# First weight pair turned between the first attention steps, and the second MLP's first product in front of the first MLP's last units

## The chip, the cores and the metric

One core of a Trainium2 chip. The metric is device time of one execution in microseconds (us); the table below has the median of 3 runs. Engines are named as the profile names them: PE is TensorE (PEld its weight loads), DVE is VectorE, ACT is ScalarE, POOL is GpSimd, SP is SyncE, which issues all transfers here.

## The reference

Three stages follow each other: a block-wise linear attention with decay (2 batches, 8 heads, 768 positions, 12 blocks of 64), an MLP (512 to 2048 to 512, leaky ReLU), and a second MLP (512 to 1024 to 512) with a SoLU and a layer norm in the middle. There are 1536 tokens.

```python
# attention, for each block b of 64 positions
intra = np.einsum('bhic,bhjc->bhij', qb, kb) * Dmask[None]
intra = np.einsum('bhij,bhjd->bhid', intra, vb)
inter = np.einsum('bhid,bhde->bhie', qb * lam_pow[None], kv_state)
out[:, :, sl] = intra + inter
kv_state = lam_block[None, :, None, None] * kv_state + np.einsum('bhsd,bhse->bhde', kb * rev_pow[None], vb)
...
# first MLP
h = x @ w_in
x = np.maximum(0.01 * h, h) @ w_out
...
# second MLP
h = x @ w_in
e = np.exp(h - h_max)
solu = h * e / (np.sum(e, axis=-1, keepdims=True) + 1e-09)
ln = (solu - mu) / np.sqrt(var + 1e-06) * g_ln
return ln @ w_out
```

The weights are of a wider type than float32 in memory; the host only regroups their bytes.

## The kernel before

**Numbers in two parts.** Every product of the MLPs is made of three: high part by high part, high by low, low by high. The activations lie in SBUF as `xhi`, `xlo` for each of three blocks of 512 tokens, the weights as tiles `wio` (first MLP), `wa`, `wb` (second MLP) with a high and a low half.

**Weights.** They arrive as raw 64-bit words (`raww`), in pairs: pair n holds column group n of `w_in` (IN) and row group n of `w_out` (OUT) of the first MLP, 512 KB each. Turning a pair into float32 parts takes four helpers: `words(n)` (two ACT operations), `convert(n)` (three DVE operations), `high(n)` (one ACT operation that rounds to the high part) and `low(n)` (one DVE subtraction). Each may be called for one half, IN or OUT.

**Attention.** There are 12 steps of one block of 64 positions for both batches. Step s has its loads (`load_step`, five transfers, 1 MB), products of scores (`scores_mm`), their mask (`scores_ev`, DVE), the new state (`scale_k`, `state_mm`, `state_ev`, with `decay_state` on POOL), the scaled queries (`scale_q`, POOL, one buffer `qs`), and the output product (`x_mm`), whose result goes to `xhi` (`x_hi`, ACT) and `xlo` (`x_lo`, DVE). Steps 0 to 3 come first and fill block 0 of the tokens; steps 4 to 11 are spread over the first MLP.

**First MLP.** A loop over 48 items: 3 blocks of tokens by 16 column groups. Item i has its first product `l1_mm` (12 matmuls into `hps`), `l1_split` (ACT: leaky ReLU in place, rounding to `ghi`; DVE: `glo`) and its second product `l2_mm` (12 matmuls into the four `acc` banks). The second product of item i - 1 stands behind the first product of item i. During items 1 to 15 the weight pairs are turned too, up to three pairs ahead. After the last item of a block, `l2_split` moves `acc` to `xhi`, `xlo`.

**Second MLP.** A loop over 12 tiles of 128 tokens: `h2_mm` (24 matmuls into two banks), `h2_norm` (maximum, ACT's exponential, DVE's products and statistics, POOL's power, DVE's last scaling: tile `e`), `ln_transpose` (8 transposes into `acc` 0 and 1), `ln_split` (ACT `lnhi`, DVE `lnlo`), and `out_mm` (24 matmuls, into `acc` 2 or 3, then a copy and a store).

**What sets the order.** Each engine runs its instructions in the order in which the code is written: at the end of the function every instruction is tied to the one before it on its engine. So all that stands ahead of a waiting instruction on its engine's list delays it. Every transfer is issued by SP, in order. PSUM has eight banks: four `acc`, two `hps`, and two that belong to attention (`aps`) and, when attention is over, to the second MLP (`bps`).

Of the kernel before, what the change touches and what calls it, by code (L numbers as in the profile page):

```python
# [16 lines left out]
P = 128  # L17
# [24 lines left out]
def fused_kernel(ctx: ExitStack, tc: tile.TileContext, att, vt, tab, cst, w_in, w_out, w_in2, w_out2, out):  # L42
# [184 lines left out]
    def load_weights(n):  # L227
        if n >= len(order):
            return
        kind, f = key = order[n]  # L230
        t = wp.tile([P, 2, 512, 2], U32, tag="w", name="raww")
        if kind == "a":
            sync.dma_start(out=t.rearrange("p h a b -> p (h a b)"), in_=w_in2[f].bitcast(U32))
        else:
            for i, src in enumerate((w_in[f], w_out[f]) if kind == "io" else (w_out2[f], w_out2[f + 1])):
                sync.dma_start(out=t[:, i].rearrange("p a b -> p (a b)"), in_=src.bitcast(U32))
                if n == 0 and i == 0:
                    load_step(NPRE - 1)
# [95 lines left out]

    et, lnt = {}, {}

    def h2_banks(t):
        return hps if t % 2 == 0 else bps

    def h2_mm(t):  # L340
        b, o = divmod(t * P, NBLK)
# [5 lines left out]
                        bank, x[b][:, k, o : o + P], w[:, s], start=(k == 0 and i == 0), stop=(k == KD - 1 and i == 2)  # L347
                    )

    def h2_norm(t, between):  # L350

        banks = h2_banks(t)
        small = sp.tile([P, 24], F32, tag="small", name="small")
# [65 lines left out]
    zero = cp.tile([P, CH], F32, name="zero")  # L419
    pool.memset(zero, 0.0)  # L420
    sync.dma_start(out=tabs, in_=tab)
    for s in range(NPRE - 1):
        load_step(s)
    for n in range(NLEAD):
        load_weights(n)
    load_step(NPRE)
    sync.dma_start(out=fix, in_=cst)
# [14 lines left out]
    scores_mm(0)  # L442
    scores_ev(0)
    state_mm(0, hps)
    state_ev(0, hps)
    x_mm(0, xb[0])
    x_hi(0, xb[0])
    x_lo(0, xb[0])

    scale_q(1, pool)  # L450
    decay_state(1, pool)
    scale_k(1, pool)
    scores_mm(1)
    scores_ev(1)
    x_mm(1, xb[1])
    state_mm(1, hps)
    x_hi(1, xb[1])
    x_lo(1, xb[1])
    state_ev(1, hps)

    decay_state(2, pool)
    scale_q(2, pool)
    scale_k(2, pool)
    scores_mm(2)
    scores_ev(2)
    x_mm(2, xb[0])
    state_mm(2, hps)
    x_hi(2, xb[0])
    words(0, IN)
    x_lo(2, xb[0])  # L470
    state_ev(2, hps)
    convert(0, IN)
    decay_state(3, pool)

    scale_q(3, pool)
    scores_mm(3)
    high(0, IN)
    low(0, IN)
    scores_ev(3)
    l1_mm((0, 0), hps[0], 0, 256)  # L480
    words(0, OUT)
    convert(0, OUT)
    x_mm(3, xb[1])
    x_hi(3, xb[1])
    x_lo(3, xb[1])
    high(0, OUT)
    low(0, OUT)
    l1_mm((0, 0), hps[0], 256, 512)
    scale_k(3, pool)
    state_mm(3, aps)  # L490
    words(1, IN)
    convert(1, IN)
    l1_split((0, 0), hps[0])
    state_ev(3, aps)
    decay_state(4, pool)
    l2_mm((0, 0))
    words(1, OUT)
    high(1, IN)
    low(1, IN)
    convert(1, OUT)  # L500
    words(2)
    high(1, OUT)
    low(1, OUT)
# [16 lines left out]
    for i, u in enumerate(items[1:], 1):  # L520
        bank = hps[i % 2]
        l1_mm(u, bank)
        s = step_at.get(i)
        before = step_at.get(i - 1)
        if s is not None:
            scale_k(s, pool)
            scale_q(s, pool)
            scores_mm(s)
        if before is not None:
            state_ev(before, aps)  # L530
            decay_state(before + 1, pool)
            x_mm(before, aps)
        l1_split(u, bank)
        high(pair_at(i, 1))
        low(pair_at(i, 1))
        if s is not None:
            scores_ev(s)
        if before is not None:
            x_hi(before, aps)
            x_lo(before, aps)  # L540
            load_step(before + 1)
        if i == 1:
            words(3)
# [94 lines left out]
```

## Time and profile before

| | us |
|---|---|
| Time, median of 3 runs | 493.92 (493.74 to 494.28) |
| Profiled execution, its own time | 494.47 |
| Its span in the trace | 492.7 |
| TensorE busy | 463.0 (94%) |
| VectorE busy | 259.5 (53%) |
| ScalarE busy | 182.4 (37%) |
| GpSimd busy | 51.1 (10%) |

The span is from the first to the last instruction; 1.8 us lie around it. Busy shares are means over all stages: the first 50 us hold four attention steps and the turning of the first weights, where several engines take turns; the rest is nearly all matmuls. A row of a list in time order gives the start, the length, engine, line, operation, output and inputs; in brackets is the idle time of the engine before it and what ended it.

### The profile page before, as it was taken

The numbers are of one execution on the slowest core, as the hardware profiler recorded it, in microseconds if no ns is written. First come the engines' busy times: TensorE is split into PE (matmuls) and PEld (weight loads), VectorE is DVE, ScalarE is ACT, GpSimd is POOL, SyncE is SP. The second block draws the span as 40 slices with busy tenths as digits, with TensorE's granted clock in tenths as the row PEclk, the third lists the DMA queues.
The fourth block names the chain that finished last, engine by engine and source line by source line (L and its number), as shares of the span: only waits on it lengthen the run. The fifth ranks groups of instructions, "written<-read, shape, count | busy, mean of one in ns | idle before, by whom it ended". The sixth has DMA issues, their size and how long they took to land.

```text
span 492.7 us, 7879 instructions
## 1 busy us (share of the span) xinstructions
PE 463.0 (94%) x3344; PEld 373.2 (76%) x3344; DVE 259.5 (53%) x412; ACT 182.4 (37%) x295; POOL 51.1 (10%) x61
## 2 busy tenths in 40 slices
PE   7474999999999999999999999999879999999997
PEld 4463777777787777777888888888658888888886
DVE  3568788788834121121131598913675666555661
ACT  2155846656423212121233677612312222222221
POOL 2603021302210202010000000000000000000000
PEclk9978899999999999999999999999989999999999
DMA  7995045634200202020005552000000000000001
GB/s 238 370 381 226 1 119 225 216 130 169 76 13 1 86 1 86 1 86 1 1 1 173 211 209 91 0 0 1 1 1 21 21 23 21 33 33 23 21 23 43
DMA packets 20243, 41.61 MB, mean 84 GB/s; under 512 B 1904, under 2 KB 11632, under 8 KB 19696
## 3 DMA queue, kind: packets, MB, share of 16 engines
q1 hardware_dynamic: 20208, 41.11, 23.8%
q8 instruction: 26, 0.43, 0.4%
q14 instruction: 9, 0.07, 0.0%
HBM read 37.95 MB, written 3.15 MB: 83 GB/s over the span
## 4 chain that ended last, share of the span: by engine, by line
PE 85%; DMA 7%; DVE 4%; issue 1%; ACT 1%; SPq 1%; POOL 0%; ACTq 0%
PE hps L311 27%; PE acc L327 27%; PE acc L404 14%; PE hps L346 6%; PE bps L346 6%; DMA raww<-in_w_out_dram 2%; DMA ld<-in_att_dram 2%; PE acc L382 2%; PE aps L187 2%; DMA raww<-in_w_in_dram 1%; PE aps L201 1%; DMA ldw<-in_att_dram 1%; PE aps L150 1%; PE aps L166 1%; DVE x L263 1%
## 5 line engine op out<-in xcount | busy, mean ns | idle before, releaser
L311 PE MATMUL hps<-xhi,wio 128*128 128x512 f32 (+1 forms) x392 | 132.8, 400 | 11.6 <-ACT wio L283 10.8
L318 DVE TENSOR_TENSOR glo<-hps,ghi 128x512 fp32r<-128x512 f32 x48 | 33.2, 691 | 126.7 <-ACT ghi L317 126.7
L327 PE MATMUL acc<-ghi,wio 128*128 128x512 f32 x384 | 97.4, 396 | 0.7 <-ACT ghi L317 0.7
L311 PEld LDWEIGHTS hps<-xhi,wio 128*128 128x128 f32 x392 | 75.0, 193 | 29.8 <-ACT wio L283 11.4
L314 ACT ACTIVATE hps<-hps 128x512 f32<-128x512 f32 x48 | 27.9, 582 | 150.1 <-PE hps L311 150.1
L327 PEld LDWEIGHTS acc<-ghi,wio 128*128 128x128 f32 x384 | 70.8, 188 | 16.7 <-ACT ghi L317 0.8
L311 PE MATMUL hps<-xlo,wio 128*128 128x512 f32 (+1 forms) x196 | 77.3, 395 | 0.1
L327 PE MATMUL acc<-glo,wio 128*128 128x512 f32 x192 | 51.4, 389 | 0.0
L404 PE MATMUL acc<-wb,lnhi 128*128 128x512 f32 (+1 forms) x208 | 48.7, 388 | 0.3 <-ACT lnhi L390 0.3
L311 PEld LDWEIGHTS hps<-xlo,wio 128*128 128x128 f32 x196 | 38.0, 194 | 7.8 <-DVE xlo L219 0.3
L404 PEld LDWEIGHTS acc<-wb,lnhi 128*128 128x128 f32 x208 | 37.4, 194 | 7.4 <-ACT lnhi L390 0.6
L327 PEld LDWEIGHTS acc<-glo,wio 128*128 128x128 f32 x192 | 36.0, 188 | 7.6
L263 DVE SCALAR_TENSOR_TENSOR x<-x,raww 128x1024 uint32<-128x1024 uint32 (+1 forms) x26 | 32.3, 1241 | 0.9
L374 POOL TENSOR_TENSOR small<-small,nhalf 128x1 f32<-128x1 f32 x12 | 6.6, 550 | 251.8 <-DVE small L373 251.8
L262 DVE SCALAR_TENSOR_TENSOR raww<-x,raww 128x1024 uint32<-128x1024 uint32 (+1 forms) x26 | 30.7, 1182 | 1.4 <-ACT raww L253 0.3
L346 PE MATMUL hps<-wa,xhi 128*128 128x512 f32 x96 | 30.2, 396 | 0.0
L346 PE MATMUL bps<-wa,xhi 128*128 128x512 f32 x96 | 30.1, 395 | 0.0
L391 DVE TENSOR_TENSOR lnlo<-acc,lnhi 128x512 fp32r<-128x512 f32 x24 | 15.5, 686 | 26.8 <-ACT lnhi L390 26.8
L317 ACT CAST ghi<-hps 128x512 fp32r<-128x512 f32 x48 | 28.2, 588 | 1.5
L253 ACT ACTIVATE raww<-raww 128x1024 uint32<-128x1024 uint16 (+1 forms) x26 | 28.0, 1077 | 0.0
L252 ACT ACTIVATE x<-raww 128x1024 f32<-128x1024 f32 (+1 forms) x26 | 27.9, 1074 | 0.0
L404 PE MATMUL acc<-wb,lnlo 128*128 128x512 f32 (+1 forms) x104 | 24.0, 373 | 0.0
(80 smaller groups left out, 500.5 us busy)
## 6 DMA issues: line engine op xcount, KB each, us to landing
raww<-in_w_out_dram SPq DMA_DIRECT2D x24, 512.0 KB, 6.5
raww<-in_w_in_dram SPq DMA_DIRECT2D x16, 512.0 KB, 7.0
raww<-in_w_in_dram SPq DMA_DIRECT2D x4, 1024.0 KB, 4.8
ld<-in_att_dram SPq DMA_DIRECT2D x8, 384.0 KB, 4.2
ld<-in_att_dram SPq DMA_DIRECT2D x24, 128.0 KB, 4.0
out_dram<-osb SPq DMA_DIRECT2D x11, 256.0 KB, 2.0
ld<-in_vt_dram SPq DMA_DIRECT2D x8, 256.0 KB, 3.7
ldw<-in_att_dram SPq DMA_DIRECT2D x4, 384.0 KB, 5.2
```

Of the source, the lines that this page charges most:

```text
L252: act.activation(x, raw[:, :, 1].bitcast(F32), AF.Copy, scale=HI_SCALE)
L253: act.activation(raw[:, :, 0], raw.bitcast(U16)[:, :, 1], AF.Copy, scale=LO_SCALE)
L262: dve.scalar_tensor_tensor(raw[:, :, 0], xu, 3, raw[:, :, 0], op0=ALU.logical_shift_left, op1=ALU.bitwise_or)
L263: dve.scalar_tensor_tensor(xu, xu, 0x80000000, raw[:, :, 0], op0=ALU.bitwise_and, op1=ALU.bitwise_or)
L311: pe.matmul(bank[:, c0:c1], w[:, s, k], x[b][:, k, c0:c1], start=(i == 0), stop=(i == len(terms) - 1))
L314: act.activation(bank, bank, AF.Prelu, alpha=0.01)
L317: act.copy(ghi, bank)
L318: dve.tensor_tensor(glo, bank, ghi.bitcast(F32), op=ALU.subtract)
L327: pe.matmul(acc[m], w[:, s, m], g, start=(f == 0 and first), stop=(f == NF - 1 and last))
L346: pe.matmul(bank, x[b][:, k, o : o + P], w[:, s], start=(k == 0 and i == 0), stop=(k == KD - 1 and i == 2))
L391: dve.tensor_tensor(lo[:, part], src, hi[:, part].bitcast(F32), op=ALU.subtract)
L404: pe.matmul(po[:, 0:n], x[:, k], w2_t["b", k][:, s, cols], start=(i == 0), stop=(i == len(terms) - 1))
```

## The change

Three things are moved; apart from the first product of item 0, which was in two parts of 256 tokens and is now in one of 512, and from `scale_k(1)`, which goes from POOL (two operations) to ACT (eight), no operation is added or removed.

1. Weight pair 0 is loaded behind step 0, ahead of steps 1 to 3 (before: its first half behind step 2, its second behind step 3).
2. The front is written in another order. Pair 0 is turned between steps 0 and 2, and pair 1 between steps 2 and 3 and behind them. `x_mm(2)` stands behind `scores_mm(3)`. Item 0's second product goes behind item 1's first.
3. The second MLP's first product of token tile 0 stands behind the second product of item 45, and its `h2_norm` behind the split of item 47. The bank pairs `hps` and `bps` change places (tile 0 uses `bps`). In the loop over tiles the output product stands ahead of the transposes, and the norm ahead of `ln_split` of the tile before; the last tile keeps the old order.

```diff
@@ load_weights
-                if n == 0 and i == 0:
-                    load_step(NPRE - 1)
@@ h2_banks
-        return hps if t % 2 == 0 else bps
+        return bps if t % 2 == 0 else hps
@@ loads
-    for s in range(NPRE - 1):
+    load_step(0)
+    load_weights(0)
+    for s in range(1, NPRE):
         load_step(s)
-    for n in range(NLEAD):
+    for n in range(1, NLEAD):
         load_weights(n)
@@ the front
     state_mm(0, hps)
+    x_mm(0, xb[0])
     state_ev(0, hps)
-    x_mm(0, xb[0])
+    words(0, IN)
     x_hi(0, xb[0])
+    words(0, OUT)
+    convert(0, IN)
     x_lo(0, xb[0])
+    decay_state(1, pool)
+    high(0, IN)
 
     scale_q(1, pool)
-    decay_state(1, pool)
-    scale_k(1, pool)
+    scale_k(1, act)
     scores_mm(1)
     scores_ev(1)
     x_mm(1, xb[1])
     state_mm(1, hps)
+    low(0, IN)
+    convert(0, OUT)
     x_hi(1, xb[1])
+    high(0, OUT)
     x_lo(1, xb[1])
     state_ev(1, hps)
...
     scores_ev(2)
-    x_mm(2, xb[0])
+    low(0, OUT)
     state_mm(2, hps)
...
+    words(1, IN)
 
     scale_q(3, pool)
     scores_mm(3)
...
+    x_mm(2, xb[0])
     scores_ev(3)
...
+    state_ev(2, hps)
+    decay_state(3, pool)
+    x_hi(2, xb[0])
+    words(1, OUT)
+    convert(1, IN)
+    x_lo(2, xb[0])
     x_mm(3, xb[1])
     x_hi(3, xb[1])
     x_lo(3, xb[1])
...
+    high(1, IN)
+    low(1, IN)
     scale_k(3, pool)
+
+    l1_mm((0, 0), hps[0])
     state_mm(3, aps)
...
+    convert(1, OUT)
+    words(2)
     l1_split((0, 0), hps[0])
+    high(1, OUT)
+    low(1, OUT)
     state_ev(3, aps)
     decay_state(4, pool)
-    l2_mm((0, 0))
...
     convert(2)
@@ the loop over items
-        if i > 1:
-            l2_mm(items[i - 1])
-            if items[i - 1][1] == NF - 1:
-                l2_split(items[i - 1][0])
+        if i == len(items) - 1:
+            h2_norm(0)
+        l2_mm(items[i - 1])
+        if items[i - 1][1] == NF - 1:
+            l2_split(items[i - 1][0])
         if s is not None:
             state_mm(s, aps)
+        if i == last:
+            att_psum.close()
+            pb = ctx.enter_context(tc.tile_pool(name="pb", bufs=1, space=bass.MemoryType.PSUM))
+            bps.extend(pb.tile([P, 512], F32, name=f"bps{j}") for j in range(2))
+        if i == len(items) - 2:
+            h2_mm(0)
@@ the loop over tiles
-    for t in range(NT):
+    for t in range(1, NT):
         h2_mm(t)
-        if t >= 1:
+        if t < NT - 1:
+            h2_norm(t)
+            if t >= 2:
+                out_mm(t - 2)
             ln_transpose(t - 1)
-        h2_norm(t, (lambda: ln_split(t - 1)) if t >= 1 else (lambda: None))
-        if t >= 2:
+            ln_split(t - 1)
+        else:
+            ln_transpose(t - 1)
+            h2_norm(t, lambda: ln_split(t - 1))
             out_mm(t - 2)
```

ScalarE's list at steps 0 and 1 (`state` and `xhi` belong to attention, `x`, `raww` and `wio` to weight pair 0, `ldw` to step 1's keys), as a piece of the difference:

```order
 L174 COPY state<-hps_87 128x256
+L250 ACTIVATE x<-raww 128x512
+L251 ACTIVATE raww<-raww 128x512
 L215 CAST xhi_92<-acc_82 128x4x64
 L215 CAST xhi_92<-acc_83 128x4x64
+L250 ACTIVATE x<-raww 128x512
+L251 ACTIVATE raww<-raww 128x512
+L281 CAST wio<-x 128x512
+L130 ACTIVATE ldw<-ldw,dmask 128x64 x8
 L215 CAST xhi_92<-acc_84 128x4x64
 L215 CAST xhi_92<-acc_85 128x4x64
```

The words of pair 0, its first rounding and the scaled keys stand now around the outputs of steps 0 and 1.

VectorE's list from step 2's state (`state`, its last part) to the rest of pair 1, after the change:

```order
L177 TENSOR_TENSOR state<-hps_87,sd 128x256
L259 TENSOR_SCALAR x<-x 128x512
L260 SCALAR_TENSOR_TENSOR raww<-x,raww 128x512
L261 SCALAR_TENSOR_TENSOR x<-x,raww 128x512
L219 TENSOR_TENSOR xlo_95<-acc_82,xhi_92 128x4x64
L219 TENSOR_TENSOR xlo_95<-acc_83,xhi_92 128x4x64
L219 TENSOR_TENSOR xlo_95<-acc_84,xhi_92 128x4x64
L219 TENSOR_TENSOR xlo_95<-acc_85,xhi_92 128x4x64
L299 TENSOR_TENSOR wio<-x,wio 128x512
```

`convert(1, IN)` stands ahead of the low parts of steps 2 and 3; before, the first half of pair 0 stood in this place, and between the two steps.

VectorE's list at the end of the first MLP, before (`glo` of item 47, then `l2_split` of block 2, then the norm of tile 0):

```order
L318 TENSOR_TENSOR glo<-hps_87,ghi 128x512
L332 TENSOR_TENSOR xlo_97<-acc_82,xhi_94 128x512
L332 TENSOR_TENSOR xlo_97<-acc_83,xhi_94 128x512
L332 TENSOR_TENSOR xlo_97<-acc_84,xhi_94 128x512
L332 TENSOR_TENSOR xlo_97<-acc_85,xhi_94 128x512
L359 TENSOR_REDUCE small<-hps_86 128x1
```

and after:

```order
L375 TENSOR_SCALAR small<-small 128x1
L376 TENSOR_SCALAR e<-e,small 128x1024
L330 TENSOR_TENSOR xlo_97<-acc_82,xhi_94 128x512
L330 TENSOR_TENSOR xlo_97<-acc_83,xhi_94 128x512
L330 TENSOR_TENSOR xlo_97<-acc_84,xhi_94 128x512
L330 TENSOR_TENSOR xlo_97<-acc_85,xhi_94 128x512
L359 TENSOR_REDUCE small<-hps_86 128x1
```

The whole norm of tile 0, up to `e`, has moved ahead of the four `xlo` pieces; behind them the norm of tile 1 begins, which now uses `hps`.

## Rows read from the trace of the kernel before

**Rows 1.** The page, busy time of each engine over the span.
```profile
PE 463.0 (94%) x3344; PEld 373.2 (76%) x3344; DVE 259.5 (53%) x412; ACT 182.4 (37%) x295; POOL 51.1 (10%) x61
```

**Rows 2.** TensorE in time order: start, length, what; gap before it and releaser.
```profile
25.49 0.58 PE L311 MATMUL hps<-xhi,wio 128*128 128x256 f32 x1 [4.55 <-ACT wio L283]
...
47.72 0.79 PE L311 MATMUL hps<-xhi,wio 128*128 128x512 f32 x1 [6.27 <-ACT wio L283]
...
55.22 0.40 PE L311 MATMUL hps<-xhi,wio 128*128 128x512 f32 x1
```

**Rows 3.** Stretches: length, busy time by engine (instructions), granted clock, DMA share, GB/s.
```profile
21.00:24.50 3.50, 0.00 (x0) 0.00 (x0) 3.38 (x4) 0.00 (x0) 3.03 (x3) 1.00 1.02 413
...
45.00:51.50 6.50, 3.78 (x9) 3.01 (x10) 5.62 (x7) 4.88 (x5) 0.00 (x0) 0.50 0.00 0
...
362.50:365.80 3.30, 3.30 (x10) 2.52 (x9) 1.19 (x4) 2.41 (x6) 0.00 (x0) 0.50 0.00 0
```

**Rows 4.** An issue of SP, its us to landing (last), the next transfer's landing.
```profile
15.42 0.43 SPq L236 DMA_DIRECT2D raww<-in_w_in_dram  x1
...
raww<-in_w_in_dram SPq DMA_DIRECT2D x1, 512.0 KB, 7.3
...
17.08 6.90 DMA raww<-in_w_out_dram
```

**Rows 5.** ScalarE (ACT) in time order, the first 55 us.
```profile
20.10 0.68 ACT L253 ACTIVATE raww<-raww 128x512 uint32<-128x512 uint16 x1
...
34.38 0.58 ACT L314 ACTIVATE hps<-hps 128x512 f32<-128x512 f32 x1 [0.53 <-PE hps L311]
...
46.62 1.04 ACT L283 CAST wio<-x 128x1024 fp32r<-128x1024 f32 x1 [2.78 <-DVE x L263]
```

**Rows 6.** VectorE (DVE) in time order, the first 55 us.
```profile
21.24 0.42 DVE L261 TENSOR_SCALAR x<-x 128x512 f32<-128x512 f32 x1
...
23.15 1.63 DVE L263 SCALAR_TENSOR_TENSOR x<-x,raww 128x512 uint32<-128x512 uint32 x1
...
26.92 0.41 DVE L261 TENSOR_SCALAR x<-x 128x512 f32<-128x512 f32 x1
...
28.15 0.69 DVE L263 SCALAR_TENSOR_TENSOR x<-x,raww 128x512 uint32<-128x512 uint32 x1
...
36.22 0.68 DVE L177 TENSOR_TENSOR state<-aps,sd 128x512 f32<-128x512 f32 x1
...
43.38 0.69 DVE L261 TENSOR_SCALAR x<-x 128x1024 f32<-128x1024 f32 x1
...
45.36 1.23 DVE L263 SCALAR_TENSOR_TENSOR x<-x,raww 128x1024 uint32<-128x1024 uint32 x1
```

**Rows 7.** GpSimd (POOL) in time order, 36 to 42 us.
```profile
36.98 1.06 POOL L142 TENSOR_TENSOR sd<-state,qpow 128x512 f32<-128x512 f32 x1 [11.13 <-DVE state L177]
38.00 1.83 POOL L132 TENSOR_TENSOR ld<-ld,dmask 128x256 f32<-128x256 f32 x2
39.80 1.74 POOL L120 TENSOR_TENSOR qs<-ld,qpow 128x512 f32<-128x512 f32 x1
```

**Rows 8.** Second MLP's start: a stretch, TensorE's, VectorE's lists, the chain of waits.
```profile
338.66:369.48 30.82, 26.01 (x114) 20.71 (x113) 21.31 (x47) 7.84 (x20) 1.11 (x2) 0.94 0.00 1
...
361.47 1.09 PE L382 MATMUL acc<-fix,e 128*128 128x128 f32 x8 [3.23 <-DVE e L376]
...
338.80 2.48 DVE L332 TENSOR_TENSOR xlo<-acc,xhi 128x512 fp32r<-128x512 f32 x4 [3.47 <-ACT xhi L331]
...
350.69 0.81 DVE L376 TENSOR_SCALAR e<-e,small 128x1024 f32<-128x1024 f32 x1
...
375.22 0.87 PE acc L382 x8
376.10 5.48 PE acc L404 x24
381.57 5.58 PE hps L346 x24
```

More of the change, by code (lines that the diff above doesn't have):

```diff
@@ L335, in fused_kernel @@
     et, lnt = {}, {}
+    bps = []
     def h2_banks(t):
-        return hps if t % 2 == 0 else bps
+        return bps if t % 2 == 0 else hps
     def h2_mm(t):
@@ L348, in h2_mm, with h2_norm @@
                     )
-    def h2_norm(t, between):
+    def h2_norm(t, between=lambda: None):
         banks = h2_banks(t)
@@ L456, in fused_kernel @@
     state_mm(1, hps)
+    low(0, IN)
+    convert(0, OUT)
     x_hi(1, xb[1])
+    high(0, OUT)
     x_lo(1, xb[1])
     state_ev(1, hps)
-    decay_state(2, pool)
     scale_q(2, pool)
     scale_k(2, pool)
+    decay_state(2, pool)
     scores_mm(2)
     scores_ev(2)
-    x_mm(2, xb[0])
+    low(0, OUT)
     state_mm(2, hps)
[L468 to L473, printed above, removed]
+    words(1, IN)
     scale_q(3, pool)
     scores_mm(3)
-    high(0, IN)
-    low(0, IN)
+    x_mm(2, xb[0])
     scores_ev(3)
-    l1_mm((0, 0), hps[0], 0, 256)
-    words(0, OUT)
-    convert(0, OUT)
+    state_ev(2, hps)
[4 more added lines that the diff above has]
+    x_lo(2, xb[0])
     x_mm(3, xb[1])
@@ L485, in fused_kernel @@
     x_lo(3, xb[1])
-    high(0, OUT)
-    low(0, OUT)
-    l1_mm((0, 0), hps[0], 256, 512)
+    high(1, IN)
+    low(1, IN)
     scale_k(3, pool)
+    l1_mm((0, 0), hps[0])
     state_mm(3, aps)
-    words(1, IN)
-    convert(1, IN)
+    convert(1, OUT)
+    words(2)
     l1_split((0, 0), hps[0])
+    high(1, OUT)
+    low(1, OUT)
     state_ev(3, aps)
     decay_state(4, pool)
-    l2_mm((0, 0))
[L497 to L503, printed above, removed]
     convert(2)
@@ L549, in fused_kernel @@
         load_weights(pair_at(i, 5))
-        if i > 1:
-            l2_mm(items[i - 1])
-            if items[i - 1][1] == NF - 1:
-                l2_split(items[i - 1][0])
+        if i == len(items) - 1:
[3 more added lines that the diff above has]
+            l2_split(items[i - 1][0])
         if s is not None:
             state_mm(s, aps)
+        if i == last:
[4 more added lines that the diff above has]
+            h2_mm(0)
     l2_mm(items[-1])
     l2_split(items[-1][0])
-    att_psum.close()
-    pb = ctx.enter_context(tc.tile_pool(name="pb", bufs=1, space=bass.MemoryType.PSUM))
-    bps = [pb.tile([P, 512], F32, name=f"bps{i}") for i in range(2)]
     NT = NTOK // P
-    for t in range(NT):
+    for t in range(1, NT):
         h2_mm(t)
-        if t >= 1:
+        if t < NT - 1:
+            h2_norm(t)
+            if t >= 2:
+                out_mm(t - 2)
             ln_transpose(t - 1)
-        h2_norm(t, (lambda: ln_split(t - 1)) if t >= 1 else (lambda: None))
-        if t >= 2:
+            ln_split(t - 1)
+        else:
+            ln_transpose(t - 1)
+            h2_norm(t, lambda: ln_split(t - 1))
             out_mm(t - 2)
```

## The prediction

> **What bounds the kernel now.** The page's first lines come first: the matrix engine is busy 463.0 of 492.7 us [rows 1], so a change of order can give back at most what lies in its gaps and in the time it works at half clock. Next the list of the matrix engine in time order, for the gaps. Two stand at the front: 4.55 us before the first product of block 0 (25.49) and 6.27 us before item 2 (47.72), both released by ScalarE rounding a turned weight to `wio` (line 283) [rows 2]. The granted clock of the stretch at 45.0 to 51.5 is 0.50, the lower of its two levels (1.2 of 2.4 GHz), and at 362.5 to 365.8 too [rows 3]: in both places a gap of some us went ahead. From 55.22 on, where item 3 starts, the front is over; I use that start as the mark of the front. The second place is the start of the second MLP: from the first product's start at 338.66 to the fourth's at 369.48 it takes 30.82 us, with the matrix engine busy 26.01 and a gap of 3.23 us that waits for VectorE's normalised `e` [rows 8]. Between these two places and behind them nothing waits long, and the change touches it only by a swap of order.
>
> **The end: second MLP's first product early.** Three first products (5.58 each), two transposes (0.87 each) and one output product (5.48) [rows 8] are 16.74 + 1.74 + 5.48 = 23.96 us of work at full clock. The stretch takes 30.82, so 6.86 are lost there. Now token tile 0's product stands two units earlier, and its normalisation runs beside the last units. Counted from its start at 0, with 0.2325 us a matmul (5.58 / 24): product to 5.6, item 47's first product (12 matmuls, 2.8) to 8.4, its `glo` 1.9 later at 10.3 (34.38 to 36.22 is this distance for item 0 [rows 5, 6]). Behind that VectorE normalises tile 0. Before, from the product's end (338.66 + 5.58 = 344.24) to the end of the last step (350.69 + 0.81 = 351.50) that took 7.26 us [rows 8], so `e` stands at 17.5; the four `xlo` pieces of `l2_split` behind it take 2.48, and the two that the transposes' banks wait for are done at 18.8. The matrix engine needs them after two second products (2.8 each) and tile 1's first product (5.58): 8.4 + 5.6 + 5.6 = 19.6. Cover left: 0.8 us. Next, VectorE starts tile 1's norm at 20.0 and ends it at 27.3, then `ln_split(0)` (two of about 0.65) at 28.6. The output product of tile 0 now starts at 19.6 + 0.9 + 5.6 = 26.1 and wants the low parts after its 16 high ones (3.7 us), at 29.8. Cover 1.2 us. In each later round the norm (7.3) and the split (1.3) must fit into 5.58 + 0.87 + 5.48 = 11.93 us; they do, and output product and transposes only change places. So all of 6.86 should go, less a little for covers under one us: I take **6.7**, with bounds 5.5 and 6.9.
>
> **The front: loads.** Weight pair 0 (two transfers of 512 KB) goes ahead of steps 1 to 3 on SP's queue. Two such transfers in a row, the halves of pair 1, land 1.28 us apart: 15.42 + 7.3 = 22.7, then 17.08 + 6.90 = 23.98 [rows 4]. So steps 1 and 2 land up to 2.6 us later and step 3 up to 1.3. What stands ahead of pair 1 is the same set of bytes in another order: its first half still lands at 22.7, and step 3, right ahead of it, no later. The second half of pair 1 and all behind it keep their places.
>
> **The front: who is last.** Pair 0 was turned from about 20 on, and is now turned between steps 0 and 2; the 4.55 us gap then loses its reason. Eight small ScalarE operations (`scale_k(1)`, 64 columns each) are added: no row is that small; the 512-column one is 0.58 [rows 5], so they cost between 0 and 4.6 us, and lie ahead of 22.7, where ScalarE would wait for pair 1 anyway. The chain is then that of pair 1, half by half, because `words(1, IN)` is in ScalarE's queue ahead of `x_hi(2)`:
> 22.7 landing; two ScalarE operations of 0.68 [rows 5], the first done at 23.4. `convert(1, IN)` on VectorE from 23.4: the same three operations took 21.24 to 24.78, 3.54 us, in one place and 26.92 to 28.84, 1.92 us, in another [rows 6]. GpSimd makes the difference: it was at work for 3.03 of the 3.5 us from 21.0 on [rows 3], and idle for 11.13 us up to 36.98 [rows 7], so through all of the second place. Now it has `scale_q(3)`, `decay(3)` and `scale_k(3)` at that time, 1.74 + 1.06 + 1.83 = 4.6 us [rows 7], since `scale_q(3)` must wait for `x_mm(2)` to have read its only buffer (about 23). I take the slow figure: 27.0. Then `x_lo(2)` and `x_lo(3)`, each about the 0.68 of a 512-column operation out of PSUM [rows 6], with gaps 1.5: 28.5. `x_hi(3)` (24.0 landing, 1.3 turning, 0.6) is done earlier. Item 0's first product, now in one piece, has 11 matmuls left from there: 2.6 us at full clock, 5.1 at half. The matrix engine has been idle since the end of `x_mm(3)` (about 25.3: 23, the 1.74 of `scale_q(3)`, and its last part), 3.2 us, and 3.23 us was followed by the half clock [rows 3, 8]; with part of it at half, item 0's product ends at **32.5** (31.1 to 33.6).
>
> From there VectorE waits: `glo(0)`, `low(1, OUT)` and `state_ev(3)` stand ahead of `convert(2)` in its queue. From the first ScalarE operation to the end of the state was 34.38 to 36.90 before [rows 5, 6], 2.5 us, and with one more 0.69 operation 3.2. `convert(2)` alone took 43.38 to 46.59, 3.2 us [rows 6]. Now GpSimd starts `decay(4)` in the same moment, with `scale_k(4)` and `scale_q(4)` behind it, 4.6 us. The slow place lost 1.62 us in 3.54, 0.46 for each us beside GpSimd: 4.6 x 0.46 = 2.1 more, 5.2 in all. `high(2)` takes 1.04 [rows 5]. Item 2 can start at 32.5 + 3.2 + 5.2 + 1.0 = 41.9, where it was 47.7. The matrix engine has 0.7 + 2.8 + 2.8 us for that time (state, item 1, second product of item 0), so a **new wait** of about 3 us stands there.
>
> From `high(2)`'s end to item 3's start was 55.22 - 47.66 = 7.56 us, with item 2 at half clock. ScalarE alone sets a floor: the words of pairs 3 and 4, four operations of the size of `high(2)` (1.04), 4.2; item 2's split, two of 0.58; `high(3)` 1.04: 6.4. I take 7.0: item 3 starts at 48.9, a gain of **6.3**. Bounds: pair 1 landing 1.3 later, half clock throughout and 7.56 give 44.4 + 7.6 = 52.0, a gain of 3.2. With neither conversion hindered and full clock: `x_lo(3)` 27.3, product to 29.9, 3.2 + 3.2 + 1.0 to 37.3, 6.4 to 43.7, a gain of 11.5. The forecast is nearer the low end since the slow conversion has a row for each of its causes.
>
> On the conversion beside GpSimd the Trainium skill ("SBUF — State Buffer", section "Who interferes with whom") says that a VectorE instruction with two SBUF inputs and a GpSimd instruction that reads SBUF take a shared port by an exclusive lock: the loser waits for the whole other instruction. The rows at 21 to 25 us agree in direction (1.63 against 0.69 us), with less than a whole GpSimd operation of 1.7 us lost each time.
>
> **The sum.** 6.3 + 6.7 = 13.0. The profiled execution took 494.47 us, 0.55 over the median of 493.92, so 481.5 on that basis and **480.9** on the median's. All bounds together: 13.0 could be 8.7 (485.2) or 18.4 (475.5).
>
> **Rivals.**
> (a) *The loads are last.* Steps 1 to 3 are late, and pair 1 with them: for it, the DMA engines are full there (share 1.02, 413 GB/s [rows 3]), and transfers that are mixed with the small ones of a step are slower. Against it, pair 1's place is unchanged. Each us late costs one: 3 us later than 22.7 leaves a gain of 3.3 at the front: 483.9.
> (b) *Conversions run free.* GpSimd happens to be idle beside them, or the clock stays up: gain 10 to 11.5 at the front, 476 to 477. For it: moments of 1 us decide this. Against: in both places GpSimd's work becomes ready at the same event as VectorE's.
> (c) *The end does not get its norm.* VectorE's norm of tile 0 is 2 us later than I count (cover 0.8), tile 1's and its split with it, and gaps with a half-clock stretch stay: 3 of the 6.7 come, 484.6. That the change then does not do what it says.
> (d) *Slower.* VectorE and GpSimd block each other operation by operation in all four conversions that now lie among the steps (0 in two halves, 1's first half, 2): 12 operations. From 1.15 us of added wait for each, all of it on the chain, 13.8 us are lost and the gain is gone: 494.7. The rows show 0.94 for the worst and 0.54 on average (1.62 / 3), and the first two conversions have time to spare before 22.7. By the rule of the Trainium skill's "SBUF — State Buffer" cited above, a wait could be as long as GpSimd's longest operation; here that is 1.83, which would be enough.
>
> **Chances and range.** The forecast 0.68, (a) 0.12, (b) 0.12, (c) 0.05, (d) 0.03. The range reaches from inside (b) over (a) and (c): 477.0 to 485.3. A measurement of this kernel can tell some 0.2% (1 us) from no change: faster 0.95, within it 0.02, slower 0.03.
>
> **What the new profile would show.** First product of block 0 near 28, in one run of 12 with part at granted clock 0.5; a conversion of 128x512 at 23 to 27 of about 3.5 us; a wait of about 3 us on `wio` before item 2 at 42, none of 6; item 3 near 49. At the end, transposes without a wait on `e`, no half clock after 60 us, rounds of 11.93. I am wrong in the front if ScalarE waits on a landing later than 24, or if the matrix engine waits again after item 3; at the end if line 382 waits on `e` or line 404 on `lnlo`.

## The result, and the profile after

| kernel | median (us) | executions, range (us) |
|---|---|---|
| before | 493.89 | 4, 493.74 to 494.28 |
| changed | 481.18 | 4, 480.41 to 483.15 |

The ratio is 0.9747, with a 95% interval of 0.9718 to 0.9777: 12.7 us less. The forecast was 480.9 (477.0 to 485.3). The profiled execution of the changed kernel took 480.41 us with a span of 478.6 (before: 494.47 and 492.7), so the two traces differ by 14.1 us in all. That is 1.4 more than the medians do: the profiled execution lay 0.6 above the median before, and 0.8 below it after.

The page after, first the busy time of each engine (before: [rows 1]):

```profile
PE 459.1 (96%) x3332; PEld 370.6 (77%) x3332; DVE 257.2 (54%) x412; ACT 184.3 (39%) x303; POOL 49.3 (10%) x59
```

TensorE in time order at the front (start, length, operation; the gap before it and its releaser), for [rows 2]. The line numbers are two lower than before: L309 is the first product of the first MLP.

```profile
12.73 0.33 PE L150 MATMUL aps<-ldw 64*64 64x64 f32 x4 [3.25 <-DMA ldw<-in_att_dram]
...
22.59 0.63 PE L187 MATMUL acc<-r,ldw 64*64 64x64 f32 x15
24.86 0.69 PE L187 MATMUL acc<-r,ldw 64*64 64x64 f32 x17 [1.64 <-issue]
25.63 0.69 PE L201 MATMUL acc<-qs,state 64*64 64x64 f32 x32
...
29.28 0.50 PE L309 MATMUL hps<-xhi,wio 128*128 128x512 f32 x1 [0.73 <-ACT xhi L215]
...
41.07 0.80 PE L309 MATMUL hps<-xhi,wio 128*128 128x512 f32 x1 [2.13 <-ACT wio L281]
...
48.21 0.40 PE L309 MATMUL hps<-xhi,wio 128*128 128x512 f32 x1
```

The gaps of 4.55 and 6.27 us are gone. In their place stand three smaller ones: 3.25 us for step 1's loads, 1.64 us inside `x_mm(2)` with nothing recorded that it waits for, and the new wait of 2.13 us before item 2. Item 3, the mark of the front, starts at 48.21 instead of 55.22: **7.0 us** come from the front.

VectorE and GpSimd at the two conversions on the chain, for [rows 6, 7]. L259 to L261 are the three operations of a `convert`:

```profile
24.09 0.43 DVE L259 TENSOR_SCALAR x<-x 128x512 f32<-128x512 f32 x1
...
25.38 0.69 DVE L261 SCALAR_TENSOR_TENSOR x<-x,raww 128x512 uint32<-128x512 uint32 x1
...
28.98 0.76 DVE L219 TENSOR_TENSOR xlo<-acc,xhi 128x256 fp32r<-128x256 f32 x2 [1.46 <-ACT xhi L215]
...
35.69 0.68 DVE L259 TENSOR_SCALAR x<-x 128x1024 f32<-128x1024 f32 x1
36.41 1.97 DVE L260 SCALAR_TENSOR_TENSOR raww<-x,raww 128x1024 uint32<-128x1024 uint32 x1
38.41 1.53 DVE L261 SCALAR_TENSOR_TENSOR x<-x,raww 128x1024 uint32<-128x1024 uint32 x1
```

```profile
26.52 1.28 POOL L120 TENSOR_TENSOR qs<-ldw,qpow 128x512 f32<-128x512 f32 x1 [3.50 <-DVE x L261]
...
28.77 1.20 POOL L132 TENSOR_TENSOR ldw<-ldw,dmask 128x256 f32<-128x256 f32 x2
...
35.85 1.44 POOL L142 TENSOR_TENSOR sd<-state,qpow 128x512 f32<-128x512 f32 x1 [5.89 <-DVE state L177]
37.26 3.16 POOL L132 TENSOR_TENSOR ld<-ld,dmask 128x256 f32<-128x256 f32 x2
```

`convert(1, IN)` ran unhindered, 24.09 to 26.07, because GpSimd did not begin until 26.52. The row names VectorE's last operation as what ended GpSimd's wait, but that operation had been done for 0.45 us. In all nine profiles with the new front and the new loads, GpSimd's `scale_q(3)` starts 0.17 to 0.20 us behind the end of `x_mm(2)` (here 25.63 + 0.69 = 26.32), so that is what it waits for. `convert(2)` was hindered, and GpSimd's scaling of step 4's keys beside it took 3.16 us, against 1.20 for the same two operations at 28.77.

Stretches of TensorE's clock (length, busy time by engine, the granted clock third from the end), for [rows 3]:

```profile
13.70:20.50 6.80, 5.77 (x154) 5.38 (x154) 4.15 (x9) 2.68 (x10) 2.66 (x3) 0.50 1.02 299
24.00:26.10 2.10, 1.15 (x47) 1.02 (x48) 1.90 (x4) 0.62 (x2) 0.00 (x0) 1.00 1.00 402
41.00:44.50 3.50, 3.43 (x8) 2.75 (x9) 3.36 (x3) 3.50 (x5) 0.65 (x1) 0.52 0.93 382
```

The lower level (0.50, 1.2 GHz) stands behind the 3.25 us gap and behind the 2.13 us wait. Item 0's product, where I had put some of it, ran at full clock, and so did all that follows 44.4 us.

At the second MLP's start, for [rows 8], VectorE's `e`, `xlo` and `lnlo`, then TensorE's first transpose, the low parts of tile 0's output product, and the fourth first product:

```profile
340.68 0.81 DVE L376 TENSOR_SCALAR e<-e,small 128x1024 f32<-128x1024 f32 x1
341.41 2.48 DVE L330 TENSOR_TENSOR xlo<-acc,xhi 128x512 fp32r<-128x512 f32 x4
...
351.37 1.28 DVE L391 TENSOR_TENSOR lnlo<-acc,lnhi 128x512 fp32r<-128x512 f32 x2
```

```profile
342.84 1.03 PE L382 MATMUL acc<-fix,e 128*128 128x128 f32 x8
...
352.95 1.98 PE L404 MATMUL acc<-wb,lnlo 128*128 128x512 f32 x8
...
355.56 0.71 PE L346 MATMUL hps<-wa,xhi 128*128 128x512 f32 x2
```

No gap stands before any of the three. From item 3 to the fourth first product it was 369.48 - 55.22 = 314.26 us; it is 355.56 - 48.21 = 307.35. So **6.9 us** come from the end, and 7.0 + 6.9 is the 13.9 of the 14.1 us between the spans. In the profiles of experiments 7, 8 and 10 this second part takes 307.37 to 307.42 us.

### The profile page after: what moved, and what is told of

Same layout as the page of the kernel before. It is cut to its first block, busy times and chain, and to the rows that moved or that the text cites. A ratio compares the mean times of both kernels' runs of the same rounds, so it can differ in the third digit from the quotient of the medians.

```text
span 478.6 us, 7874 instructions
## 1 busy us (share of the span) xinstructions
PE 459.1 (96%) x3332; PEld 370.6 (77%) x3332; DVE 257.2 (54%) x412; ACT 184.3 (39%) x303; POOL 49.3 (10%) x59
## 4 chain that ended last, share of the span: by engine, by line
PE 91%; issue 2%; DVE 1%; ACT 1%; POOL 1%; ACTq 0%; POOLq 0%
PE hps L309 28%; PE acc L325 28%; PE acc L404 14%; PE bps L346 7%; PE hps L346 7%; PE acc L382 2%; PE aps L187 2%; PE aps L201 1%; PE aps L150 1%; PE aps L166 1%; DVE raww L260 0%; DVE x L261 0%; POOL sd L142 0%; POOL qs L120 0%; ACT wio L281 0%
## 5 line engine op out<-in xcount | busy, mean ns | idle before, releaser
L309 PE MATMUL hps<-xhi,wio 128*128 128x512 f32 x384 | 130.8, 401 | 2.9 <-ACT wio L281 2.1
L309 PEld LDWEIGHTS hps<-xhi,wio 128*128 128x128 f32 x384 | 72.7, 189 | 21.1 <-ACT wio L281 2.5
L309 PE MATMUL hps<-xlo,wio 128*128 128x512 f32 x192 | 76.1, 396 | 0.0
L404 PE MATMUL acc<-wb,lnhi 128*128 128x512 f32 (+1 forms) x208 | 46.1, 374 | 0.3 <-ACT lnhi L390 0.3
L309 PEld LDWEIGHTS hps<-xlo,wio 128*128 128x128 f32 x192 | 36.6, 191 | 8.0 <-DVE xlo L219 0.3
L261 DVE SCALAR_TENSOR_TENSOR x<-x,raww 128x1024 uint32<-128x1024 uint32 (+1 forms) x26 | 31.0, 1192 | 0.9
L299 DVE TENSOR_TENSOR wio<-x,wio 128x1024 fp32r<-128x1024 f32 (+1 forms) x18 | 20.5, 1141 | 3.9 <-ACT wio L281 3.8
```

Source lines behind the costliest of these rows:

```text
L261: dve.scalar_tensor_tensor(xu, xu, 0x80000000, raw[:, :, 0], op0=ALU.bitwise_and, op1=ALU.bitwise_or)
L299: dve.tensor_tensor(t[:, 1, halves], x[:, halves], t[:, 0, halves].bitcast(F32), op=ALU.subtract)
L309: pe.matmul(bank[:, c0:c1], w[:, s, k], x[b][:, k, c0:c1], start=(i == 0), stop=(i == len(terms) - 1))
L404: pe.matmul(po[:, 0:n], x[:, k], w2_t["b", k][:, s, cols], start=(i == 0), stop=(i == len(terms) - 1))
```

## The experiments

**1. The front alone.** The changed kernel with the old end: the bank pairs, the tile loop and tile 0's place as before.

```diff
 def h2_banks(t):
-        return bps if t % 2 == 0 else hps
+        return hps if t % 2 == 0 else bps
 the loop over items
-        if i == len(items) - 1:
-            h2_norm(0)
...
-        if i == len(items) - 2:
-            h2_mm(0)
...
```

> The changed kernel with its end put back: the second MLP's first product and the loop over tiles stand as before; the front and the loads are the new ones. Theory (two gains that add up, front 7.0 and end 6.9 by the two traces): item 3 starts near 48.2, the second MLP's start takes its 30.8 us again, and the time is 493.9 - 7.0 = 486.9. Rival (the front's lead is given back later, because the loop over items waits for a transfer or for VectorE): item 3 is early but the last item is not, 490 or more.

Measured: 488.28 us (487.21 to 488.54), ratio 0.9875 (0.9845 to 0.9904), span 486.3: 5.8 us less than the 494.12 of before in that comparison. TensorE's waits (engine, tile and line, what it waited for, total us, times, longest):

```profile
PE acc L380 <- DVE e L374: 4.8, 2, 3.2
```

The two waits on `e` are back, so they belong to the end's part. Both marks that the theory named were missed. Item 3 started at 50.43 here and not at 48.2, since item 0 started at 29.88 and its product ran partly at half clock (granted clock 0.63 from 31.0 to 35.3). From the first first product (333.88) to the fourth (363.10) it was 29.22 us, against 30.82 of before [rows 8]: the same 4.8 us of waits, but no half clock such as that from 362.5 to 365.8 there [rows 3]. So of the 6.9 us that the end gains in the two profiles, some 1.6 are that half-clock stretch, which not every execution need have. The rival is out: from item 3 to the first first product it was 283.45 us, before 338.66 - 55.22 = 283.44, so the loop over items gives nothing of the front's lead back.

**2. The end alone.** The old front and the new end.

```diff
 def h2_banks(t):
-        return hps if t % 2 == 0 else bps
+        return bps if t % 2 == 0 else hps
 the loop over items
+        if i == len(items) - 1:
+            h2_norm(0)
...
+        if i == len(items) - 2:
+            h2_mm(0)
...
```

> The kernel before with the new end alone; front and loads as before. Theory: item 3 at 55.2 as before, no wait of a transpose on e, 493.9 - 6.9 = 487.0. Rival (the lead at the end hangs on the new front or on the banks being exchanged there): 489 or more.

Measured: 488.59 us (487.24 to 488.63), ratio 0.9878 (0.9848 to 0.9909), span 486.8. The front's gaps stand as before (4.49 us before block 0, and the one before item 2 below), and item 3 starts late:

```profile
48.84 0.79 PE L311 MATMUL hps<-xhi,wio 128*128 128x512 f32 x1 [6.28 <-ACT wio L283]
...
56.44 0.40 PE L311 MATMUL hps<-xhi,wio 128*128 128x512 f32 x1
```

From there to the fourth first product (363.79) it is 307.35 us, to the hundredth what the changed kernel takes. The time gained only 5.5 where 6.9 was expected. For the profiled execution (488.63 us) the marks say why: it was 1.2 us later at item 3 than the profiled one of before. Both parts alone give 5.8 + 5.5 = 11.3, both together 12.7; the medians of such runs are not sharper than about 1 us.

**3. The old loads under the new front.** The weight pair 0 goes back behind step 2, its second half behind step 3; the order of all other work is the changed one.

```diff
-    load_step(0)
-    load_weights(0)
-    for s in range(1, NPRE):
+    for s in range(NPRE - 1):
         load_step(s)
-    for n in range(1, NLEAD):
+    for n in range(NLEAD):
         load_weights(n)
```

> The changed kernel with the loads in the old order (pair 0's first half behind step 2, its second behind step 3); the instructions of the engines stay as changed. Theory (the load order carries the front, because ScalarE's queue now has pair 0's words ahead of the outputs of step 0 and step 1): ScalarE waits for 17.1 and 21.5, step 1's keys are scaled 8 us later, item 0 starts some 7 us later: 488, slower than the changed kernel. Rival (pair 1's landing at 23.4 is what the front waits for, and pair 0 only has to be there before it): 481 to 483.

Measured: 486.73 us (486.43 to 488.35), ratio 0.9854 (0.9822 to 0.9886). ScalarE and TensorE in time order:

```profile
17.98 0.66 ACT L252 ACTIVATE x<-raww 128x512 f32<-128x512 f32 x1 [8.76 <-DMA raww<-in_w_in_dram]
```

```profile
21.97 1.97 PE L187 MATMUL acc<-r,ldw 64*64 64x64 f32 x32 [10.04 <-DVE r L155]
...
36.37 0.49 PE L311 MATMUL hps<-xhi,wio 128*128 128x512 f32 x1 [0.73 <-ACT xhi L215]
```

With pair 0's words ahead of attention's work in ScalarE's queue, a late pair 0 holds up all that stands behind: 8.76 us on ScalarE, 10.04 on TensorE, item 0 at 36.37 instead of 29.28. Item 3 starts at 54.39, 6.2 later than in the changed kernel and only 0.8 ahead of the kernel before. The new order of the front needs the new order of the loads; some 5.5 of the front's 7 us hang on it (486.73 - 481.18). The other half of the question, the new loads under the old order, was not run, and the moves within the front were not told apart either.

**4. GpSimd out of the way of `convert(2)`.** A one-element operation on GpSimd that reads a result of `convert(3)` stands ahead of `decay_state(4)`, so GpSimd begins step 4's scaling only behind that conversion.

```diff
     state_ev(3, aps)
-    decay_state(4, pool)
     convert(2)
 the loop over items, item 1
             convert(3)
+            pool.tensor_tensor(one, xs_t[3][:, 1, 511:512], nhalf, op=ALU.mult)
+            decay_state(4, pool)
             words(4)
```

> The changed kernel with GpSimd's work for step 4 (decay, keys, queries) held back: a one-column GpSimd operation that reads what convert(3) wrote stands ahead of it. Theory (convert(2) lost 1.1 us to GpSimd and stands on the path): convert(2) takes 3.2 us, not 4.26; high(2) ends 1.1 earlier, the matrix engine's wait ahead of item 2 falls from 2.1 to 1.0 and item 3 starts 1.0 to 1.7 earlier: 479.8. Rival (the half clock and ScalarE's words set item 3's start): convert(2) is shorter, item 3 is not earlier, 481.

Measured: 483.0 us (479.29 to 483.82), ratio 0.9772 (0.9739 to 0.9805), not told apart from the changed kernel's. The profile is of the fastest of the five executions (479.29); the other four took 482.86 to 483.82. VectorE at `convert(2)`, at `convert(4)` and at step 4's mask (L155), then TensorE:

```profile
36.72 1.22 DVE L261 SCALAR_TENSOR_TENSOR x<-x,raww 128x1024 uint32<-128x1024 uint32 x1
...
47.64 2.19 DVE L260 SCALAR_TENSOR_TENSOR raww<-x,raww 128x1024 uint32<-128x1024 uint32 x1
...
53.40 0.68 DVE L155 TENSOR_TENSOR r<-aps,dmask 128x512 f32<-128x512 f32 x1
```

```profile
39.08 0.51 PE L309 MATMUL hps<-xhi,wio 128*128 128x512 f32 x1 [1.08 <-ACT wio L281]
...
54.19 0.69 PE L166 MATMUL aps<-ld 64*64 64x64 f32 x32 [2.27 <-issue]
```

The cause of the slow conversion is confirmed: without GpSimd beside it `convert(2)` takes 3.2 us instead of 4.25, the wait before item 2 is 1.08, and item 3 starts 16.95 us behind item 0's start (18.93 in the changed kernel). But GpSimd's work then falls on `convert(4)` (2.19 for an operation of 1.23), and at step 4's state product TensorE stops for 2.27 us. The row gives no releaser for this stop, but the product writes the banks that the mask reads, and starts 0.11 us behind the mask's end (53.40 + 0.68 = 54.08; the same 0.11 in the changed kernel): TensorE waits for VectorE's list, in which the mask stands behind the slowed conversion. From item 0's start to that product it is 25.86 us against 26.03: the gain is given back ten microseconds later.

**5 and 9. `convert(2)` earlier.** It moves behind `words(2)`, ahead of item 0's split, into a time in which GpSimd is idle anyway. It ran twice.

```diff
     words(2)
+    convert(2)
     l1_split((0, 0), hps[0])
...
     decay_state(4, pool)
-    convert(2)
```

> VectorE does convert(2) directly behind the turn of the state's words, ahead of item 0's lo terms, instead of behind them and behind state_ev(3). Theory A (item 2 waits for high(2), and high(2) only for convert(2)'s place in VectorE's row): convert(2) runs at about 32.3 to 35.5 us, item 0's lo terms come 3 us later, high(2) ends near 38.5, TensorE no longer waits before item 2 (2.13 us in the changed kernel) and does not stand at half clock in it, item 3 starts 2.5 to 3.5 us earlier, near 45.2. If this reaches the end, the time is near 478; if GpSimd's work then lands beside convert(4), as with GpSimd's gate, 481. Theory B (TensorE's wait only moves to item 0's lo products, which wait for glo behind convert(2)): a wait of 2 to 3 us on VectorE ahead of l2(0) or state_mm(3), item 3 at 48, and 481 to 482.

> The kernel with convert(2) early once more, in five rounds, beside the changed kernel on the same chip. In its first profile TensorE went from item 0's start to step 4's first state product in 23.92 us, in the changed kernel in 26.03: 2.1 us less, while item 0 itself started 1.7 us later there because the loads landed later. Theory A (the later loads were chance): over ten executions the median is 1 to 2.5 us under the changed kernel's. Theory B (what the path gains is given back before item 0, whatever the loads do): the two medians agree within 0.7 us.

Measured: 480.09 us (478.15 to 481.32, 4 executions), ratio 0.9708 (0.9671 to 0.9745), and 480.07 (478.80 to 481.05, 5 executions), ratio 0.9707 (0.9674 to 0.974). The profile of the first, VectorE and TensorE:

```profile
34.67 1.23 DVE L260 SCALAR_TENSOR_TENSOR raww<-x,raww 128x1024 uint32<-128x1024 uint32 x1
35.93 1.23 DVE L261 SCALAR_TENSOR_TENSOR x<-x,raww 128x1024 uint32<-128x1024 uint32 x1
...
42.88 2.15 DVE L260 SCALAR_TENSOR_TENSOR raww<-x,raww 128x1024 uint32<-128x1024 uint32 x1
```

```profile
30.94 0.50 PE L309 MATMUL hps<-xhi,wio 128*128 128x512 f32 x1 [0.73 <-ACT xhi L215]
...
47.42 0.50 PE L309 MATMUL hps<-xhi,wio 128*128 128x512 f32 x1 [1.29 <-ACT wio L281]
...
54.86 0.69 PE L166 MATMUL aps<-ld 64*64 64x64 f32 x32 [0.82 <-issue]
```

`convert(2)` is undisturbed, no wait stands before item 2, and 1.29 of those 2.13 us come back before item 3, since `convert(3)` now lies beside GpSimd (2.15); in the second profile it does not, and 0.23 us is left there. From item 0's start to step 4's state product it is 23.92 us, in the second profile 53.66 - 29.23 = 24.43, against 26.03 and 26.11 in two profiles of the changed kernel: about 1.9 us shorter. The gain is kept: from item 0's start to the second MLP's first product it is 292.13 and 292.57 us, against 294.13 and 294.27. The times show less of it. All nine executions have a median of 480.07, the lowest of this study, and the ten of the changed kernel 480.95; that is 0.9 us, and against experiment 10 alone 0.7, between what the two theories expected and at the edge of what these runs can tell. Two things scatter by more than that. The loads put item 0's start at 29.2 in one profile and at 30.9 in the other. And the time at half clock differs between executions: in experiment 10, the two with a mean granted clock of 0.993 took 479.25 and 479.52 us, the two with 0.982 took 483.22 and 483.27.

**6. Both, and step 4's words later.**

```diff
     words(2)
+    convert(2)
...
-    decay_state(4, pool)
-    convert(2)
 the loop over items, item 1
             convert(3)
-            words(4)
+            pool.tensor_tensor(one, xs_t[3][:, 1, 511:512], nhalf, op=ALU.mult)
+            decay_state(4, pool)
 and item 2, behind high(3)
+            if i == 2:
+                words(4)
```

> convert(2) early as in the run before, GpSimd's scaling for step 4 held until convert(3) is through, and the turn of step 4's words behind high(3) in item 2 instead of ahead of it. If the gain of the early convert(2) was given back at state_mm(4) because GpSimd lies beside convert(4), this gives the same as it or is worse: 480 to 483. If the row of ScalarE (words ahead of high(3)) is what is late next, item 3 starts without its wait (0.42 us in the run with GpSimd's gate) and the time is near 477.5.

Measured: 482.59 us (478.27 to 483.51), ratio 0.9733 (0.9672 to 0.9793). Item 3 starts at 46.69 without any wait, but step 4's state product at 55.69 behind a gap of 2.49 us, 25.57 behind item 0's start. Behind that gap TensorE stood at the lower clock (0.50 from 55.7 to 60.0), and from step 4's state product to step 5's it took 23.81 us, 2.8 more than in the changed kernel (21.03). Holding GpSimd back only moves the collision, here as in experiment 4.

**7. Four warm matmuls fewer** at the start of the program (`NWARM` 8 instead of 12). This asks what the 1.64 us inside `x_mm(2)` are.

```diff
-NWARM = 12
+NWARM = 8
```

> Four fewer warm matmuls at the start, nothing else. In the changed kernel TensorE breaks off inside x_mm(2) behind its 15th matmul for 1.64 us, with no wait recorded. Theory A (instructions run out: the break stands at a fixed count of TensorE's instructions): the break moves to behind about the 19th matmul, or into the next group. Theory B (it is tied to the data or the transfers of x_mm(2)): it stays behind the 15th. Either way the time is within 1 us of the changed kernel, 480 to 483.

Measured: 481.15 us (480.76 to 481.55, 2 executions), ratio 0.9733 (0.9691 to 0.9774). TensorE:

```profile
22.57 0.74 PE L187 MATMUL acc<-r,ldw 64*64 64x64 f32 x19
25.01 0.57 PE L187 MATMUL acc<-r,ldw 64*64 64x64 f32 x13 [1.70 <-issue]
```

The break moved from behind the 15th matmul to behind the 19th: it stands at a count of TensorE's instructions, not at a datum. Nor does it stand at a time: in the seven profiles with twelve warm matmuls and a break, it comes behind the 15th matmul each time, but begins anywhere from 22.6 to 25.8 us.

**8. Warm matmuls in the gap for step 1.** Twelve of them behind `x_mm(0)`, where TensorE waits 3.25 us in the changed kernel.

```diff
     x_mm(0, xb[0])
+    for _ in range(12):
+        pe.matmul(acc[3], c1.to_broadcast([P, P]), c1.to_broadcast([P, 512]), start=True, stop=True)
     state_ev(0, hps)
```

> Twelve more warm matmuls behind x_mm(0), where TensorE waits 3.25 us for step 1 in the changed kernel and stands at half clock from 13.7 to 20.5 us. Theory A (that half clock is covered, since step 2's and the first weights' landings set x_mm(2) and convert(1,IN)): the clock is full there, item 0 starts at most 0.5 us earlier than 29.28, and the time is 480 to 482. Theory B (it costs what TensorE does in it, about 1.8 us): item 0 starts 1.5 to 2 us earlier and the time is near 479.

Measured: 483.14 us (481.49 and 484.79), ratio 0.9773 (0.9712 to 0.9834), span 479.7. Neither theory had it. The stretch that was at half clock, then VectorE, GpSimd and TensorE:

```profile
13.70:20.50 6.80, 3.94 (x158) 3.39 (x158) 5.62 (x11) 2.77 (x10) 3.99 (x4) 1.00 1.07 290
```

```profile
24.05 1.30 DVE L259 TENSOR_SCALAR x<-x 128x512 f32<-128x512 f32 x1 [0.76 <-ACT x L250]
25.43 1.38 DVE L260 SCALAR_TENSOR_TENSOR raww<-x,raww 128x512 uint32<-128x512 uint32 x1
26.85 0.99 DVE L261 SCALAR_TENSOR_TENSOR x<-x,raww 128x512 uint32<-128x512 uint32 x1
27.76 1.40 DVE L219 TENSOR_TENSOR xlo<-acc,xhi 128x256 fp32r<-128x256 f32 x4
```

```profile
23.79 1.27 POOL L120 TENSOR_TENSOR qs<-ldw,qpow 128x512 f32<-128x512 f32 x1 [2.09 <-PE acc L201]
25.02 1.25 POOL L142 TENSOR_TENSOR sd<-state,qpow 128x512 f32<-128x512 f32 x1
26.22 2.10 POOL L132 TENSOR_TENSOR ldw<-ldw,dmask 128x256 f32<-128x256 f32 x2
```

```profile
26.83 0.50 PE L309 MATMUL hps<-xhi,wio 128*128 128x512 f32 x1 [1.02 <-ACT xhi L215]
29.22 0.50 PE L309 MATMUL hps<-xlo,wio 128*128 128x512 f32 x1 [1.88 <-DVE xlo L219]
...
49.27 0.40 PE L309 MATMUL hps<-xhi,wio 128*128 128x512 f32 x1
```

The clock was full from 13.7 to 20.5 (1.00 instead of 0.50), `x_mm(2)` ran without a break and was done near 23.6, and item 0 did start 2.45 us earlier. But now GpSimd's `scale_q(3)` began at 23.79 and its three operations lay beside `convert(1, IN)`: 3.79 us instead of 1.98. So the low parts were done only 0.6 us earlier (29.16 against 29.74), and item 0's second matmul waited 1.88 us for them. A half-clock stretch followed inside the product (0.61 from 29.2 to 33.6), and item 3 started at 49.27, 1.1 later than in the changed kernel. With two executions the times themselves are not told apart. In the profile, the early half clock and the break in `x_mm(2)` cost the changed kernel nothing on balance, not because other work covered them, but because by holding GpSimd back they kept a conversion free.

**10. The changed kernel again**, on the same chip as the second run of experiment 9.

> The changed kernel once more, without any edit, in five rounds, as the measure for the run before. Its median within 1 us of 481.2, item 0 at 29 to 31 us, the wait before item 2 at 2.1 us, and convert(1) of w_in not slowed wherever x_mm(2) breaks off; if the break does not occur, convert(1) of w_in takes near 3.8 us beside GpSimd, as with the warm matmuls behind x_mm(0).

Measured: 480.81 us (479.25 to 483.27, 6 executions), ratio 0.9733 (0.9693 to 0.9773). Item 0 at 29.52, the break in `x_mm(2)` 1.43 us, the wait before item 2 2.09, item 3 at 48.52: a second profile of the changed kernel takes the course of the first.

## Why the prediction was right, step by step

The time, the sum and both of its terms held: 6.3 was expected of the front and 7.0 came, 6.7 of the end and 6.9 came. The medians differ by 12.7, a little less than the 13.0 that was expected, and the marks of the two profiles by 13.9, a little more. None of the signs of being wrong came: ScalarE waited for no landing later than 23.39, no transpose waited for `e` and no output product for `lnlo`, and TensorE's stops behind item 3 are those that the kernel before has too (0.59 us at each state product, 0.3 at the last `lnhi`). But inside the front several steps were off, and they cancelled.

| step of the prediction | said (us) | profile after (us) |
|---|---|---|
| pair 1's first half lands | 22.7 | by 23.39 |
| `convert(1, IN)` ends | 27.0 | 26.07 |
| `x_lo(3)` ends | 28.5 | 29.74 |
| item 0's product ends | 32.5 | 32.6 |
| from there to `convert(2)` | 3.2 | 3.1 |
| `convert(2)` | 5.2 | 4.25 |
| `high(2)` ends | 41.9 | 41.0 |
| wait before item 2 | about 3 | 2.13 |
| `high(2)`'s end to item 3 | 7.0 | 7.2 |
| item 3 starts | 48.9 | 48.2 |

**Item 0's product at 32.5: right by luck.** I had taken the slow figure for `convert(1, IN)`, because `scale_q(3)` would become ready at about 23, with the end of `x_mm(2)`. `x_mm(2)` broke off for 1.64 us and ended near 26.3, GpSimd waited for it, and the conversion ran free; but `scale_q(3)`, and with it `x_mm(3)`, came 3 us later than I counted, and its low parts 1.2 us later. Half clock, of which I had put some into the product, was absent there. The errors cancelled to 0.1 us. Experiment 8 shows the course that I had worked out: `x_mm(2)` through at 23.6, the conversion 3.79 us (I said 3.54), half clock in the product, its end at 33.6, item 3 at 49.3 (I said 48.9). Experiment 1 shows a third, with the break and the half clock in the product both: item 3 at 50.4. Over five profiles with this front, experiments 1, 7, 8 and 10 and the first, item 3 started at 48.2 to 50.4. What the prediction had as a single path is a set of paths that end within about 2 us of one another.

**The conversion beside GpSimd.** The mechanism was right, and experiment 4 shows it by taking GpSimd away. The size was not: the term 4.6 x 0.46 = 2.1 measured 1.04 (1.97 and 1.53 us for two operations that take 1.23 alone), since GpSimd's third operation began at 40.38, behind the conversion, and the price for each us side by side was 0.29 (1.04 of the 3.6 us from 36.4 to 40.0) and not 0.46. Nor is it one price: in experiment 8 `convert(1, IN)` lost 1.81 of its 3.79 us, 0.48 for each. The trace shows the other side too: GpSimd's pair of key scalings took 3.16 instead of 1.20 us. The rule of the Trainium skill, "SBUF — State Buffer", section "Who interferes with whom", that the loser waits for the whole of the other's instruction, is not contradicted by this, and no row shows one such wait by itself. But the price that I gave it, 1.83 us, is that of a row of two operations [rows 7]; undisturbed, one key scaling is 0.60 us and GpSimd's longest single operation 1.28 (at 26.52). VectorE's two slowed operations lost 0.74 and 0.30 us, GpSimd's two scalings 1.96 together, beside VectorE operations that take 1.23 alone. So rival (d), which needed 1.15 us for each of VectorE's twelve operations, was far off; the largest loss of one in any profile here was 0.98 (2.21 for 1.23, experiment 6).

**The new wait** stands where it was put, smaller by about the same 0.9 us. Experiment 5 shows that it was one of order: `convert(2)` ahead of item 0's split removes it.

**The loads.** Rival (a) asked for pair 1 to land 3 us late; it landed at most 0.7 late. Step 1, which I had 2.6 us later at no price, left TensorE idle for 3.25 us and at half clock behind. By experiment 8 that did have a price, 2.45 us at item 0's start, which came back only because it kept GpSimd off a conversion. That no price held in the sum is luck too. The eight small operations of `scale_k(1)` on ScalarE took 2.03 us (bounds 0 to 4.6), ahead of a wait of 3.27 us on the landing, as said.

**The end.** The covers were thinner than counted, and held. From tile 0's first product at 323.41, `e` stood at 18.1 (said 17.5), TensorE wanted it at 19.4 (19.6); the first half of the four `xlo` pieces, which frees the transposes' banks, was done at about 19.2 (18.8), so some 0.2 us of cover were left and not 0.8. The low parts were ready at 29.2 (28.6) and wanted at 29.5 (29.8): 0.3 instead of 1.2. With 0.2 to 0.3 us more on VectorE, TensorE would have begun to wait, which is the way to rival (c). The rounds take 11.9 us, as said. The 6.9 holds 1.6 of half clock that before had in its profile, as experiment 1 shows; the waits themselves are 4.8. In an execution of before without that stretch the end's term would be some 5.3, just under its lower bound of 5.5.

## What to carry to other kernels

Ask of every operation that is moved whether the other engine's work, which becomes ready at the same event, still does so: here a late TensorE group made one conversion fast and a prompt one made it slow, with item 3 no earlier for it. Where two engines hinder each other, moving work into a time in which the other is idle anyway (experiment 5) kept the gain up to the second MLP; holding the other engine back (experiments 4 and 6) moves the collision to the next conversion. And mark two or three points of the trace at which the work done is the same, such as item 3's start, and compare those: they told the end's part of the gain to 0.1 us, where ten executions of the changed kernel lie up to 4 us apart.

## What the runs showed of the hardware

TensorE stopped for 0.6 to 1.8 us inside `x_mm(2)`, with no semaphore behind it, in every profile with the new loads but that of experiment 8, and in none with the old ones. Four instructions less ahead of it moved it by four matmuls. What fits in time is a packet of 16 KB on the DMA queue for instructions. In the changed kernel one starts at 22.22 us and ends near 23.41, TensorE stops at 23.22 and goes on at 24.86. In each of the eight profiles with the stop, TensorE goes on 1.2 to 1.5 us behind the end of such a packet, though that moment lies anywhere from 23.9 to 26.4. In experiment 8, which has no stop, the packet runs earlier, from 19.15 to 20.37. The queue's line (packets, MB, share of 16 engines), in the changed kernel between 22 and 23 us, then in experiment 8 between 19 and 20:

```profile
q8 instruction: 1, 0.02, 7.5%
...
q8 instruction: 1, 0.02, 7.6%
```

The kernel's own transfers fill the engines between 15 and 30 us in both (share 1.01 and 1.04). Instructions that come late behind full DMA engines would explain the count, the time at which TensorE goes on, and that it came with the new loads. The queue has 26 such packets in the whole execution, 0.43 MB; only TensorE, with 3332 matmuls and as many weight loads, has instructions by the thousand, so they are most likely its own. All this is argued and not shown: the profile does not name the engine that a packet is for, and no run here took the transfers away at that point.
